# Computing the last 64 tokens of four sequences from two matmuls on a block-diagonal layout of their weights

## The chip, the cores and the metric

The kernel runs on one core of a Trainium2 chip. Time is the device time of one execution in microseconds (us); times given for a kernel are the median of several executions. A profile shows one execution; its span is the time from the first to the last recorded instruction. Engines are called as in the profile: PE (TensorE matmuls; PEld are its weight loads), DVE (VectorE), ACT (ScalarE), POOL (GpSimd) and SP (SyncE, which here issues DMAs).

## The reference, cut to what matters

A gated recurrence over four sequences of 5056 tokens with 256 channels is followed by a soft mixture of experts over all 20224 tokens, with 8 experts of 4 slots each (32 slots).

```python
sig = 1.0 / (1.0 + np.exp(-f_logit))
f = lower_bound + (1.0 - lower_bound) * sig
for t in range(S):
    h = f[:, t] * h + (1.0 - f[:, t]) * x[:, t]
    y[:, t] = h
...
logits = x @ phi                            # x is y as (20224, 256); 32 slots
d = softmax of logits over the tokens       # slot inputs: d.T @ x
slot_out[e] = np.maximum(slot_input[e] @ w1[e], 0.0) @ w2[e]
c = softmax of logits over the 32 slots
return c @ slot_out                         # (20224, 256), float32
```

What the change touches is the last line, for the last 64 tokens of each sequence.

## The kernel before

Everything is laid out by hand; each engine executes its instructions in the order in which the source issues them.

**Stage 1 (to about 120 us)** streams `x` and `f_logit` in units of one sequence by 512 tokens (`load`, L210), computes gates on ACT, their products with x on POOL, transposes on PE, and the recurrence as scans on DVE (L319). Logits come out of PE with the slots on the partitions: partition `32 b + s` holds slot s of sequence b. Their exponentials lie in `etall`, 128 partitions by 5056 tokens, in bf16 (L120). PE also adds up the slot inputs (`slot_ps`).

**Stage 2 (to about 144 us)** runs the experts while the last weights arrive through POOL's DMA queue (`load_w`, L135). Among this, `row_sums` (L394) adds the 32 exponentials of each token with matmuls against `ones`, whose first four columns hold ones on the 32 partitions of one sequence each and whose other columns are all ones. The sums go into PSUM and their reciprocals into `rrow`. Matmuls that only keep PE busy (`spin`, `narrow`, L150 to L159) stand at several places. The last operations of the stage form `slot_out` (L750), the expert outputs with slots on partitions, repeated for the four sequences; `slot_bd` (L759), made of it on POOL, has two column halves of 256, in which every other sequence's rows are zero.

**Stage 3 (from 143.5 us)** multiplies the exponentials by the expert outputs, scales each row by its reciprocal sum, and stores. The tokens of a sequence are cut into `blocks`: two of 2048 tokens (16 a partition) and one of 896 (7 a partition); 64 tokens are left over (`L`). Three early rows are stored first (`total` and `early`, L753 to L757). Then follow `pieces` for the first block of the last sequence, `whole` and `couple` for the last block, `rest` for the left-over tokens, and `whole` and `couple` for the other blocks (L853 to L863). `couple` handles two sequences in one matmul of 512 columns; DVE and ACT take turns in scaling (`by_vector`, `by_scalar`). All stores are issued by SP in this order. Tiles `ob` and `oc` have three buffers each; a fourth use waits for the store of the first.

The left-over tokens before: `left_over` (L406) copies each sequence's last 64 columns of `etall` into `left`, 64 tokens by 2, where the second index is the sequence's parity and the other half stays zero. `rest` (L836) does two matmuls, one for each pair of sequences, over 64 partitions and 512 columns. Each leaves two halves, which ACT copies and DVE adds, so that partition `2 t + u` holds token t of one of the two sequences. One DVE instruction then scales both, and SP issues two stores with one row of 256 values (1 KB) a partition. Their row sums are one matmul against `pair_ones` (L402).

Of the kernel before, what the change touches and what calls it, by code (L numbers as in the profile page):

```python
# [9 lines left out]
F32 = mybir.dt.float32  # L10
BF16 = mybir.dt.bfloat16
AX = mybir.AxisListType
ALU = mybir.AluOpType
# [5 lines left out]
def kernel(  # L19
# [10 lines left out]
    nc = tc.nc  # L30
    B, S, D = x.shape
    E = moe_w1.shape[0]
    F = moe_w1.shape[2]
    NS = moe_phi.shape[1]
    SPE = NS // E
    P = 128
    DC = D // P
    FC = F // P
    R = 4
    G = P * R  # L40
    n_grp = (S + G - 1) // G
# [15 lines left out]
    L = used(odd) - P * R3  # L57
# [9 lines left out]
    consts = ctx.enter_context(tc.tile_pool(name="consts", bufs=1))  # L67
# [20 lines left out]
    ones = consts.tile([P, P], BF16, name="ones")  # L88
# [2 lines left out]
    for b in range(B):  # L91
        nc.vector.memset(ones[ds(b * NS, NS), ds(b, 1)], 1.0)

    pair_ones = consts.tile([P, B // 2], BF16, name="pair_ones")
    nc.vector.memset(pair_ones, 0.0)
    for j in range(B // 2):
        nc.vector.memset(pair_ones[ds(j * 2 * NS, 2 * NS), ds(j, 1)], 1.0)

    parity = consts.tile([P, 2], F32, name="parity")
    nc.vector.memset(parity, 0.0)  # L100
    for b in range(B):
# [16 lines left out]
    store = ctx.enter_context(tc.tile_pool(name="store", bufs=1))  # L118
    PAD = 48
    etall = store.tile([P, S + PAD], BF16, name="etall")[:, :S]  # L120
    rrow = store.tile([P, n_grp * R, B], F32, name="rrow")
    left = store.tile([P, L, 2], BF16, name="left")
    nc.vector.memset(left, 0.0)
    csum = store.tile([P, n_grp], F32, name="csum")
    nc.vector.memset(csum, 0.0)
# [2 lines left out]
    slot_bd = store.tile([P, 2, D], BF16, name="slot_bd")  # L128
    slot_out = store.tile([P, D], BF16, name="slot_out")
# [25 lines left out]
    def narrow(dst, k):  # L155
        for i in range(k):
            nc.tensor.matmul(dst[ds(i % B * NS, NS), ds(0, D)], w1_sb[0][:, 0, ds(0, NS)],
                             w1_sb[0][:, 0, ds(0, D)], start=True, stop=True,
                             skip_group_check=True)  # L159
# [8 lines left out]
    with tc.tile_pool(name="sp2", bufs=3) as sp2, \  # L168
# [225 lines left out]
        def row_sums(i):  # L394

            t0, n_r = blocks[i]
            ew = etall[:, ds(t0, P * n_r)].rearrange("s (p r) -> s p r", r=n_r)
            for r in range(n_r):
                nc.tensor.matmul(sums[:, ds((t0 // P + r) * B, P)], ew[:, :, r], ones,
                                 start=True, stop=True, skip_group_check=True)  # L400
            if i == len(blocks) - 1:
                nc.tensor.matmul(rs_ps[:, n_grp * R - 1, ds(0, B // 2)],  # L402
                                 left.rearrange("s t u -> s (t u)"), pair_ones,
                                 start=True, stop=True, skip_group_check=True)

        def left_over():  # L406
            for b in range(B):
                k = ds(b * NS, NS)
                nc.gpsimd.tensor_copy(left[k, :, b % 2], etall[k, ds(S - L, L)])

        def slots(g):
            n_p = rows(g)
# [72 lines left out]
        for n in range(n_unit):  # L485
# [14 lines left out]
            else:  # L500
# [40 lines left out]
                if n == n_unit - 2:  # L541
                    tail = psp.tile([P, 2, G], F32, name="tail", tag="sp")
                    sums = tail[:, 0]
                    rs_ps = sums[:, ds(0, n_grp * R * B)].rearrange(
                        "p (q b) -> p q b", b=B)
# [44 lines left out]
        slots(odd)  # L590
        late_slots()
        spin(tail[:, 1], 2, D)
        narrow(tail[:, 1], 8)
        slot_sb = hpool.tile([P, G, DC], BF16, name="slot_sb", tag="h")
        slot_sb = slot_sb.rearrange("p t o -> p (t o)").bitcast(F32)[:, ds(0, D)]
        nc.vector.tensor_copy(slot_sb, slot_ps)
# [2 lines left out]
        for o in range(DC):  # L599
            nc.tensor.matmul(sin_ps[:, o], slot_v[:, o], rep[:, 0],  # L600
                             start=True, stop=True, skip_group_check=True)
# [3 lines left out]
    with tc.tile_pool(name="ew", bufs=1) as ew, \  # L605
# [116 lines left out]
        nc.vector.tensor_copy(total, sum_ps)  # L722
        k = len(blocks) - 1
        nc.vector.reciprocal(rrow[:, k * wide_r:q], rs_ps[:, k * wide_r:q])
        nc.vector.reciprocal(rrow[:, q, ds(0, B // 2)], rs_ps[:, q, ds(0, B // 2)])
        nc.tensor.matmul(so_ps, rep2, total, start=True, stop=False, skip_group_check=True)

        def last_chunk(fc):
# [34 lines left out]
    with tc.tile_pool(name="osb", bufs=3, reuse_waits="tile") as osb:  # L763

        def by_vector(ob, op, scale):
            nc.vector.tensor_tensor(ob, op, scale.broadcast_to(list(ob.shape)), ALU.mult)  # L766

        def by_scalar(ob, op, scale):
            for i in range(ob.shape[1]):
                nc.scalar.activation(ob[:, i], op[:, i], ACT.Copy, scale=scale[:, i])  # L770

        def share(op, i, b, r, k):
            t0, n_r = blocks[i]
            ew = etall[ds(b * NS, NS), ds(t0, P * n_r)].rearrange("s (p r) -> s p r", r=n_r)
            for j in range(k):
                nc.tensor.matmul(op[:, j], ew[:, :, r + j], slot_out[ds(b * NS, NS)],  # L776
                                 start=True, stop=True, skip_group_check=True)

        def scale_of(i, b, r, k):
            return rrow[:, ds(blocks[i][0] // P + r, k), ds(b, 1)]  # L780

        def rows_of(i, b):
            t0, n_r = blocks[i]
            return out[ds(b * S + t0, P * n_r)].rearrange("(p r) d -> p r d", r=n_r)

        pout = ctx.enter_context(
            tc.tile_pool(name="pout", bufs=8, space=PSUM, reuse_waits="tile"))

        def bank():
            return pout.tile([P, 2, D], F32, name="op", tag="op")  # L790

        def pieces(i, b):
            dst = rows_of(i, b)
            ob = osb.tile([P, blocks[i][1], D], F32, name="ob", tag="ob")
            for r, ks in ((3, (1, 1)), (5, (1, 1)), (7, (1, 1)), (9, (2, 2)), (13, (2, 1))):
                q = r
                for k, by in zip(ks, (by_vector, by_scalar)):
                    op = bank()
                    share(op, i, b, q, k)
                    by(ob[:, ds(q, k)], op[:, ds(0, k)], scale_of(i, b, q, k))  # L800
                    q += k
                nc.sync.dma_start(out=dst[:, ds(r, q - r)], in_=ob[:, ds(r, q - r)])

        turn = [0]

        def next_engine():
            turn[0] += 1
            return turn[0] % 2

        def whole(i, b):  # L810
            n_r = blocks[i][1]
            ob = osb.tile([P, n_r, D], F32, name="ob", tag="ob")
            for r in range(0, n_r, 2):
                k = min(2, n_r - r)
                op = bank()
                share(op, i, b, r, k)
                (by_scalar, by_vector)[next_engine()](
                    ob[:, ds(r, k)], op[:, ds(0, k)], scale_of(i, b, r, k))
            nc.sync.dma_start(out=rows_of(i, b), in_=ob)

        def couple(i, j):
            t0, n_r = blocks[i]
            ew = etall[ds(j * 2 * NS, 2 * NS), ds(t0, P * n_r)].rearrange(
                "s (p r) -> s p r", r=n_r)
            ob = osb.tile([P, 2, n_r, D], F32, name="oc", tag="oc")
            for r in range(n_r):
                op = bank()
                nc.tensor.matmul(op.rearrange("p u d -> p (u d)"), ew[:, :, r],  # L828
                                 slot_bd[ds(j * 2 * NS, 2 * NS)].rearrange("s u d -> s (u d)"),
                                 start=True, stop=True, skip_group_check=True)  # L830
                (by_scalar, by_vector)[next_engine()](
                    ob[:, :, r], op, rrow[:, t0 // P + r, ds(2 * j, 2)].unsqueeze(2))
            for u in range(2):
                nc.sync.dma_start(out=rows_of(i, 2 * j + u), in_=ob[:, u])

        def rest():  # L836
            n_p = B // 2
            ob = osb.tile([P, n_p, D], F32, name="ob", tag="ob")
            dst = out.rearrange("(b t) d -> t b d", b=B)
            for j in range(n_p):  # L840
                k = ds(j * 2 * NS, 2 * NS)
                op = bank()
                nc.tensor.matmul(op.rearrange("p u d -> p (u d)"),
                                 left[k].rearrange("s t u -> s (t u)"),
                                 slot_bd[k].rearrange("s u d -> s (u d)"),
                                 start=True, stop=True, skip_group_check=True)
                nc.scalar.copy(ob[:, j], op[:, 0])
                nc.vector.tensor_tensor(ob[:, j], ob[:, j], op[:, 1], ALU.add)
            by_vector(ob, ob, rrow[:, n_grp * R - 1, ds(0, n_p)].unsqueeze(2))
            for j in range(n_p):  # L850
                nc.sync.dma_start(out=dst[ds(S - L, L), ds(2 * j, 2)], in_=ob[:, j])

        pieces(0, B - 1)  # L853
        end = len(blocks) - 1
        whole(end, 0)
        whole(end, 1)
        couple(end, 1)
        rest()
        whole(0, B - 2)
        for i in range(end):  # L860
            for j in range(B // 2):
                if i or j < B // 2 - 1:
                    couple(i, j)  # L863
# [30 lines left out]
```

## Time and profile before

| | |
|---|---|
| median of 3 runs | 197.58 us (197.51 to 197.93) |
| the profiled execution | 197.61 us, span 195.8 us |
| busy share of the span | PE 77%, DVE 75%, ACT 72%, POOL 52% |
| mean granted PE clock | 0.857 of full |
| read from and written to HBM | 58.23 MB and 20.71 MB |
| first store issued / last store packet starts | 143.50 us / about 193.4 us |

The page gives each engine's busy time, the span in 40 slices of 4.9 us, the chain of work that ended last, groups of instructions by source line and operand, and the DMA issues with size and the time until they had landed. A group reads: line, engine, operation, output and inputs, partitions by elements, count, busy time, mean. The trace behind the page also answers for stretches of time (busy time of each engine, clock, DMA share and GB/s), as a timeline, and by tile. A DMA store or load is split into packets of one contiguous run each, spread over 16 DMA engines.

Where tiles lie in a partition is fixed when the program is built; tiles are rounded up to 32 bytes. The tiles that matter, in bytes from the partition's start:

| tile | before | after |
|---|---|---|
| `pair_ones` (4 bytes used) | 19488 | none |
| `etall` | 19552 | 19520 |
| `left` | 30400, 256 bytes | 30368, 512 bytes |
| `slot_out` | 31744 | 31968 |
| `w1_sb0` | 32256 | 32480 |
| `f_t`, first buffer | 89600 | 89824 |
| `x_t`, first buffer | 114176 | 114400 |
| `ob` of `pieces` | 65024 | 65248 |
| `oc`, first buffer | 81408 | 81632 |
| `total` | 147680 | 147904 |
| `early` | 148704 | 148928 |

All buffers of `f_t`, `x_t`, `w1_sb`, `w2_sb`, `ob` and `oc` start on multiples of 512 before, and 224 bytes past one after. 48 unused columns of bf16 (`PAD`, L119) stand behind `etall` in both.

### The profile page before, as it was taken

The page shows a single profiled execution, that of the slowest core. Times are in us where ns is not written, and L with a number is a line of the kernel's source. Part 1 is how long each engine was busy: PE and PEld are TensorE (multiplying, and loading weights), DVE is VectorE, ACT ScalarE, POOL GpSimd, SP SyncE. Part 2 cuts the span into 40 slices and gives each one's busy share as a digit, 9 for nine tenths or more (in the row PEclk, how much of TensorE's full clock was granted, in tenths as well). Part 3 has the DMA queues.
Part 4 walks back from the last instruction along what each step waited for, and adds up shares of the span by engine and source line. Part 5 has one row for each costly group of instructions (what it writes and reads, how often), then busy time and mean ns, then how long its engine had stood idle before and what let it go on. Part 6 is the DMA issues. An engine that isn't in the chain of part 4 may idle for free.

```text
span 195.8 us, 3290 instructions
## 1 busy us (share of the span) xinstructions
PE 151.2 (77%) x1209; PEld 105.9 (54%) x1209; DVE 145.9 (75%) x188; ACT 141.6 (72%) x198; POOL 101.5 (52%) x79
## 2 busy tenths in 40 slices
PE   0589498987998979899797987998889999950000
PEld 0367377775785757667585766556573533410000
DVE  2669869989699999999999999544289888950000
ACT  3698687799889998999987799434089799960000
POOL 2489578874997789874969979253030000000000
PEclk9999979998799999999999999999995555555555
DMA  5999999999999999999999999999949999999994
GB/s 203 395 419 421 428 428 423 425 428 365 372 428 427 408 327 427 420 421 340 369 420 421 260 215 213 214 213 214 172 180 417 425 430 428 425 432 442 435 442 181
DMA packets 14305, 70.75 MB, mean 361 GB/s; under 512 B 1601, under 2 KB 2882, under 8 KB 10322
## 3 DMA queue, kind: packets, MB, share of 16 engines
q1 hardware_dynamic: 11520, 62.13, 76.5%
q0 software_dynamic: 2768, 8.42, 21.7%
q8 instruction: 9, 0.15, 0.3%
q14 instruction: 6, 0.05, 0.1%
q10 hardware_dynamic: 2, 0.00, 0.0%
HBM read 58.23 MB, written 20.71 MB: 403 GB/s over the span
## 4 chain that ended last, share of the span: by engine, by line
PE 33%; DMA 23%; DVE 18%; POOL 7%; issue 5%; ACT 2%; SPq 0%; POOLq 0%; ACTq 0%; DVEq 0%
DMA x_t<-in_x_dram 15%; DVE h L319 13%; PE op L828 11%; DMA w_sb<-in_moe_w_dram 9%; POOL u_t L252 6%; PE hp L332 4%; PE up L273 3%; DVE ht L351 3%; PE sp L267 3%; PE op L776 3%; PE lg L365 2%; PE slot_ps L189 2%; POOL w_sb L147 1%; DVE et L389 1%; ACT ob L770 1%
## 5 line engine op out<-in xcount | busy, mean ns | idle before, releaser
L252 POOL TENSOR_TENSOR u_t<-s_t,x_t 128x1024 bf16<-128x1024 bf16 (+1 forms) x39 | 82.5, 2131 | 22.8 <-ACT s_t L241 13.5
L319 DVE TENSOR_TENSOR_SCAN h<-a,h,up 128x512 bf16<-128x512 f32 (+1 forms) x72 | 86.8, 1252 | 5.1 <-PE up L273 2.9
L241 ACT ACTIVATE s_t<-f_t 128x2048 bf16<-128x2048 f32 (+2 forms) x23 | 38.3, 1668 | 4.8 <-DMA f_t<-in_f_logit_dram 4.8
L332 PE MATMUL hp<-ident_f,h 128*128 128x128 f32 (+1 forms) x160 | 29.7, 311 | 8.2 <-DVE ht L351 6.8
L332 PEld LDWEIGHTS hp<-ident_f,h 128*128 128x128 f32 (+1 forms) x160 | 23.5, 207 | 18.8 <-DVE ht L351 13.2
L267 PE MATMUL sp<-ident_f,s_t 128*128 128x128 f32 x144 | 23.0, 307 | 6.5 <-ACT s_t L241 4.6
L301 ACT ACTIVATE a<-sp,lbs 128x1024 f32<-128x1024 bf16 x24 | 25.4, 1115 | 1.1 <-PE sp L267 1.0
L267 PEld LDWEIGHTS sp<-ident_f,s_t 128*128 128x128 f32 x144 | 18.6, 158 | 8.4 <-ACT s_t L241 5.2
L828 PE MATMUL op<-slot_bd,etall 64*128 64x512 bf16 x55 | 22.7, 626 | 0.0
L770 ACT ACTIVATE oc<-op,rrow 128x256 f32<-128x256 f32 x54 | 21.4, 505 | 0.2
L766 DVE TENSOR_TENSOR oc<-op,rrow 128x512 f32<-128x512 f32 x28 | 18.8, 688 | 3.3 <-PE op L828 3.2
L308 ACT ACTIVATE a<-sp,lbs 128x512 f32<-128x512 bf16 (+2 forms) x22 | 17.8, 858 | 4.6 <-PE sp L267 4.2
L273 PE MATMUL up<-ident_f,u_t 64*128 64x64 f32 x192 | 17.9, 232 | 2.1 <-POOL u_t L252 2.1
L273 PEld LDWEIGHTS up<-ident_f,u_t 64*128 64x128 f32 x192 | 14.2, 141 | 6.1 <-POOL u_t L252 2.5
L189 PE MATMUL slot_ps<-rep,ident_f 128*128 128x256 f32 x52 | 16.9, 419 | 0.0
L351 ACT COPY ht<-hp 128x512 f32<-128x512 f32 (+1 forms) x20 | 11.7, 583 | 5.6 <-PE hp L332 5.5
L828 PEld LDWEIGHTS <-etall 64*128 64x128 bf16 x55 | 8.3, 158 | 13.4 <-issue 12.9
L351 DVE COPY ht<-hp 128x512 f32<-128x512 f32 (+1 forms) x20 | 13.3, 667 | 0.8 <-PE hp L332 0.8
L319 DVE TENSOR_TENSOR_SCAN h<-a,up 128x512 bf16<-128x512 f32 x8 | 9.4, 1211 | 2.8 <-ACT a L308 1.9
L267 PE MATMUL up<-ident_f,u_t 128*128 128x128 f32 x48 | 9.5, 331 | 0.8 <-POOL u_t L252 0.8
L365 PE MATMUL lg<-h,phi 128*32 128x512 bf16 (+1 forms) x80 | 9.4, 389 | 0.3 <-ACT et L389 0.2
L189 PEld LDWEIGHTS slot_ps<-rep,ident_f 128*128 128x128 f32 x52 | 8.3, 194 | 1.6 <-issue 0.6
(132 smaller groups left out, 154.1 us busy)
## 6 DMA issues: line engine op xcount, KB each, us to landing
f_t<-in_f_logit_dram SPq DMA_DIRECT2D x12, 1024.0 KB, 12.1
x_t<-in_x_dram SPq DMA_DIRECT2D x12, 1024.0 KB, 11.5
out_dram<-oc SPq DMA_DIRECT2D x6, 2048.0 KB, 12.3
w_sb<-in_moe_w_dram POOLq DMA_DIRECT2D x14, 512.0 KB, 10.2
f_t<-in_f_logit_dram SPq DMA_DIRECT2D x12, 512.0 KB, 8.5
x_t<-in_x_dram SPq DMA_DIRECT2D x12, 512.0 KB, 9.7
out_dram<-ob SPq DMA_DIRECT2D x1, 2048.0 KB, 9.2
out_dram<-ob SPq DMA_DIRECT2D x2, 896.0 KB, 5.6
```

The costliest lines, as they stand in the source:

```text
L189: nc.tensor.matmul(slot_bank[:, 1], ident_f, wide_rep, start=False, stop=False, skip_group_check=True)
L241: nc.scalar.activation(s_t, f_t, ACT.Sigmoid, scale=-1.0)
L252: nc.gpsimd.tensor_tensor(uts[n][:, :r], s_t[:, :r], x_t[:, :r], ALU.mult)
L267: nc.tensor.transpose(ps[:, :, r], t[:, r], ident_f)
L273: nc.tensor.transpose(v[:, :, r], t(r)[k].bitcast(F32), ident_f[k, k])
L301: nc.scalar.activation(a, sp[:, :, :, :, o], ACT.Identity, scale=nomlb[:, ds(o, 1)], bias=1.0)
L319: nc.vector.tensor_tensor_scan(h[:, :T, o], decays[n // 2, o][:, n % 2, :T], up[:, :T, o], hs[number(g - 1, b)][:, ds(used(g - 1) - 1, 1), ...
L332: nc.tensor.transpose(hp[:n_p, r], hw[:, :n_p, r], ident_f)
L351: copy(hts[g][:n_p, b].rearrange("p r d -> p (r d)").bitcast(F32), hps.pop(n)[:n_p].rearrange("p r c -> p (r c)"))
L766: nc.vector.tensor_tensor(ob, op, scale.broadcast_to(list(ob.shape)), ALU.mult)
L770: nc.scalar.activation(ob[:, i], op[:, i], ACT.Copy, scale=scale[:, i])
L828: nc.tensor.matmul(op.rearrange("p u d -> p (u d)"), ew[:, :, r], slot_bd[ds(j * 2 * NS, 2 * NS)].rearrange("s u d -> s (u d)"), start=Tru ...
```

## The change

`left` becomes 128 partitions by 2 by 32 by 4: for each parity r of the token, 32 tokens by 4 sequences, where partition `32 b + s` is filled only at index b. So one matmul over all 128 partitions against `slot_out` gives, for token parity r, the outputs of 32 tokens of all four sequences, with token and sequence on the partitions: partition `4 t + b`. Two matmuls of 256 columns (r = 0 and 1) fill both halves of one PSUM bank, one DVE instruction scales them, and one store writes 2 KB, two neighbouring tokens, from each partition. Nothing is left to be added, so ACT's copies and DVE's additions go, and `rest` no longer reads `slot_bd`. The row sums are two matmuls against column B of `ones` (a column of all ones) in place of one against `pair_ones`, which goes with its memsets. POOL's copies in `left_over` read every other token. One of eight `narrow` matmuls behind the slot inputs goes.

```diff
-    pair_ones = consts.tile([P, B // 2], BF16, name="pair_ones")
-    nc.vector.memset(pair_ones, 0.0)
-    for j in range(B // 2):
-        nc.vector.memset(pair_ones[ds(j * 2 * NS, 2 * NS), ds(j, 1)], 1.0)
...
-    left = store.tile([P, L, 2], BF16, name="left")
+    left = store.tile([P, 2, L // 2, B], BF16, name="left")
     nc.vector.memset(left, 0.0)
...
             if i == len(blocks) - 1:
-                nc.tensor.matmul(rs_ps[:, n_grp * R - 1, ds(0, B // 2)],
-                                 left.rearrange("s t u -> s (t u)"), pair_ones,
-                                 start=True, stop=True, skip_group_check=True)
+                for r in range(2):
+                    nc.tensor.matmul(rs_ps[:, n_grp * R - 1, ds(r, 1)],
+                                     left[:, r].rearrange("s t b -> s (t b)"),
+                                     ones[:, ds(B, 1)],
+                                     start=True, stop=True, skip_group_check=True)
...
-                nc.gpsimd.tensor_copy(left[k, :, b % 2], etall[k, ds(S - L, L)])
+                nc.gpsimd.tensor_copy(left[k, :, :, b], etall[k, ds(S - L, L)].rearrange(
+                    "s (t r) -> s r t", r=2))
...
-        narrow(tail[:, 1], 8)
+        narrow(tail[:, 1], 7)
...
-        nc.vector.reciprocal(rrow[:, q, ds(0, B // 2)], rs_ps[:, q, ds(0, B // 2)])
+        nc.vector.reciprocal(rrow[:, q, ds(0, 2)], rs_ps[:, q, ds(0, 2)])
...
         def rest():
-            n_p = B // 2
-            ob = osb.tile([P, n_p, D], F32, name="ob", tag="ob")
-            dst = out.rearrange("(b t) d -> t b d", b=B)
-            for j in range(n_p):
-                k = ds(j * 2 * NS, 2 * NS)
-                op = bank()
-                nc.tensor.matmul(op.rearrange("p u d -> p (u d)"),
-                                 left[k].rearrange("s t u -> s (t u)"),
-                                 slot_bd[k].rearrange("s u d -> s (u d)"),
+            ob = osb.tile([P, 2, D], F32, name="ob", tag="ob")
+            op = bank()
+            for r in range(2):
+                nc.tensor.matmul(op[:, r], left[:, r].rearrange("s t b -> s (t b)"), slot_out,
                                  start=True, stop=True, skip_group_check=True)
-                nc.scalar.copy(ob[:, j], op[:, 0])
-                nc.vector.tensor_tensor(ob[:, j], ob[:, j], op[:, 1], ALU.add)
-            by_vector(ob, ob, rrow[:, n_grp * R - 1, ds(0, n_p)].unsqueeze(2))
-            for j in range(n_p):
-                nc.sync.dma_start(out=dst[ds(S - L, L), ds(2 * j, 2)], in_=ob[:, j])
+            by_vector(ob, op, rrow[:, n_grp * R - 1, ds(0, 2)].unsqueeze(2))
+            dst = out.rearrange("(b t) d -> b t d", b=B)[:, ds(S - L, L)]
+            nc.sync.dma_start(out=dst.rearrange("b (t r) d -> t b (r d)", r=2),
+                              in_=ob.rearrange("p r d -> p (r d)"))
```

## The prediction, made before the changed kernel had run

> **What bounds the kernel now.** I read the windows by stage first, because a share over the whole span mixes stages. The columns after the engines are granted clock, busy share of the 16 DMA engines and GB/s moved.
>
> ```profile
> 0.70:34.60 33.90, 23.67 (x130) 18.81 (x131) 25.00 (x44) 24.60 (x27) 22.80 (x18) 0.95 0.97 396
> 34.60:110.00 75.40, 67.92 (x618) 52.38 (x618) 71.61 (x69) 68.85 (x66) 60.08 (x34) 0.98 1.02 396
> 119.50:142.00 22.50, 20.09 (x296) 13.19 (x294) 11.41 (x22) 8.83 (x18) 8.30 (x16) 1.00 1.04 204
> 145.00:193.40 48.40, 28.83 (x91) 12.41 (x87) 26.36 (x42) 28.27 (x75) 0.73 (x1) 0.52 1.01 425
> ```
>
> The DMA engines are full in the loads (to 110 us), in the weights (119 to 142) and in the stores (145 to 193.4). In the store stage no compute engine is busy for more than 0.60 of the time (PE, 28.83 of 48.40). So whatever the changed `rest` saves in compute there is worth nothing unless it changes what the DMA engines do. Next the timeline of the edited place:
>
> ```profile
> 150.39 0.63 PE L843 MATMUL op<-slot_bd,left 64*128 64x512 bf16 x1
> 150.93 0.65 ACT L847 COPY ob<-op 128x256 f32<-128x256 f32 x2
> ...
> 152.12 0.69 DVE L766 TENSOR_TENSOR ob<-ob,rrow 128x512 f32<-128x512 f32 x1
> 152.76 3.03 ACT L770 ACTIVATE ob<-op,rrow 128x256 f32<-128x256 f32 x8 [1.18 <-DMA out_dram<-ob]
> 153.08 2.56 SPq L851 DMA_DIRECT2D out_dram<-ob  x2
> ```
>
> After `rest`, ACT waits 1.18 us for an earlier `ob` store to land: the next rows are held by the stores, not by `rest`. Its own 1 KB packets move only at 158.5 to 159.5, 5.7 us after issue, behind queued stores.
>
> Last, the rates of single stores:
>
> ```profile
> 144.50:144.70 0.20, 0.20 (x4) 0.20 (x3) 0.20 (x1) 0.20 (x2) 0.20 (x1) 1.00 1.00 333
> 145.15:145.65 0.50, 0.50 (x8) 0.50 (x7) 0.50 (x2) 0.50 (x3) 0.50 (x1) 1.00 1.02 385
> 146.00:146.50 0.50, 0.34 (x4) 0.34 (x4) 0.50 (x2) 0.50 (x3) 0.00 (x0) 1.00 1.06 406
> 146.50:147.00 0.50, 0.50 (x5) 0.42 (x4) 0.50 (x2) 0.50 (x2) 0.00 (x0) 0.56 1.10 426
> 147.00:147.50 0.50, 0.50 (x4) 0.11 (x2) 0.50 (x2) 0.50 (x3) 0.00 (x0) 0.50 1.03 397
> 158.60:159.10 0.50, 0.50 (x2) 0.16 (x1) 0.34 (x2) 0.50 (x3) 0.00 (x0) 0.50 1.05 367
> ```
>
> These are, in order, `total` (1 KB packets), `early` (2 KB), three windows of `pieces` (2 KB) and `rest` (1 KB). `total` and `early` start 224 bytes past a multiple of 512 in their partition (147680 and 148704); all `ob` tiles start on a multiple of 512. Time per packet on one engine is 16 x bytes / rate. For 2 KB it is 85.1 ns in `early` against 79.9 ns in `pieces` (mean 410 GB/s); for 1 KB it is 49.2 ns in `total` against 44.6 ns in `rest`. Both pairs differ by about 5 ns, on the same side.
>
> **The change part by part.** The profiled execution took 197.61 us (span 195.8, so 1.8 around it); the median is 197.58. I add to 197.6.
>
> *Row sums (L402).* One more 128x128 weight load and matmul stand between the row sums and the chain `so_ps`, `slot_out`, first store. The load takes 0.10 us (140.41 to 140.51), and PE takes up L726 at 140.62, when `total` is just there (DVE L722 ends at 140.56). The second load fits that gap; its matmul may push L726. Between 0 and 0.17 us (L402's own matmul); I take 0.05, by the row sums of L399 at 1.22 us for 16.
>
> *One narrow matmul fewer (L157).* 0.05 us of PE at 128 us (8 in 0.40). PE then waits 1.18 us for weights at 137.87, which hides it; without that cover, -0.05. The clock is granted at 1.00 from 126.08 to 146.56 in every stretch, even with PE busy 2.23 of 3.41 us, so I price a clock loss at nothing.
>
> *Constants and POOL.* `pair_ones` loses three DVE memsets (0.06 + 0.17 us) and the memset of `left` doubles from 0.11 us, all before 2.5 us; DVE then waits 2.71 us for x_t. The four POOL copies (258 ns each, from 133.0) now read with a step of 2. At 258 to twice that they end by 135.1, and the first reader is at 140.41. All nothing.
>
> *`rest` itself.* PE goes from 2 x 0.43 us to 2 x 0.23 (16 rows of L776 in 3.63); ACT loses 0.65, DVE 0.75, SP one issue of 1.28. The following rows still wait at 152.76 for the same store, so ACT's wait becomes 1.8 us in place of 1.18. `whole(0, 2)` is then issued at 155.8 as now, after its last ACT row. The first matmul no longer needs `slot_bd` but `slot_out`, ready since 143.7. Nothing; were the DMA backlog gone, at most the 0.75 of DVE would show.
>
> *Its store.* 16 packets of 1 KB per engine (16 x 44.6 = 0.71 us) become 8 of 2 KB: 8 x 79.9 = 0.64, or 8 x 85.1 = 0.68 off the multiple. In a full queue this counts: -0.03 to -0.07; I take -0.03.
>
> *What is not in the diff's lines: addresses.* Dropping `pair_ones` frees 32 bytes a partition and `left` grows from 256 to 512, so every tile allocated behind it moves by +224. Before, in the program's layout, f_t, x_t, w1_sb, w2_sb, `ob` and `oc` all start on multiples of 512 (f_t 89600, `ob` 65024, `oc` 81408); after, all stand 224 past one, exactly where `early` stands now. `total` and `early` go from 224 to 448 and stay off.
>
> Store packets behind `early`, per engine (a store of 128 rows gives each of the 16 engines 8): `pieces` five stores, 40; the last block four stores of 7 KB rows, 32; the other blocks seven stores of 16 KB rows, 56. Together 128, and at 5 ns 0.64 us. Bounds: 0 (the two slow stores were the first in an empty queue) and 5.2 x 128 = 0.67; no misaligned 7 or 16 KB packet is in the trace. I take 0.64, because two sizes show the same extra.
>
> Here a page bears on it. The Trainium skill, "DMA: Bandwidth & Descriptors", section "How a descriptor splits into AXI transactions", says that a transaction starts on a 256 B boundary, so an unaligned descriptor begins below its start and pays for unused 32 B beats. At 224 these are 7 beats; at 79.9 ns for the 64 beats of 2 KB that is an estimated 8.7 ns, 1.1 us over 128 packets, and 198.7 by the same sum. The trace agrees in sign, with 5 ns in place of 8.7; its 198.7 lies in the first case's own range below. Whether writes into the core pay too the section does not say.
>
> Loads write to the shifted addresses; no row shows an off-multiple load. From the issue list each engine has 192 packets of 8 KB, 192 of 4 KB, 64 of 3 KB and 32 of 1 KB, 480 in all: 0 to 480 x 5.2 = 2.5 us. A misaligned start was seen only where the core is read, so I take 0 and keep 2.5 as the bound. The weight packets (4 KB cast to bf16) take twice a plain one because twice the bytes are read; 0 too.
>
> Sum: 197.6 + 0.05 - 0.03 + 0.64 = 198.3.
>
> **The rivals.**
>
> *Loads pay as well.* For it: the load stage runs at a DMA share of 0.97 and 1.02, so nothing hides a slower packet. Against: no row, and DVE is nearly as full (71.61 of 75.40). 197.6 + 0.66 + 2.5 = 200.8 at most, half of the loads' part 199.5.
>
> *Addresses cost nothing.* The 5 ns would be the start of an empty queue, and longer packets would hide it. Then 197.6 + 0.05 - 0.07 = 197.6, no change.
>
> *Faster: the last engine catches up.* The end is set by one DMA engine that is one packet behind:
>
> ```profile
> 193.00:193.20 0.20, 0.00 (x0) 0.00 (x0) 0.00 (x0) 0.00 (x0) 0.00 (x0) 0.50 0.00 0
> 193.20:193.40 0.20, 0.00 (x0) 0.00 (x0) 0.00 (x0) 0.00 (x0) 0.00 (x0) 0.50 0.23 82
> ```
>
> 82 GB/s in 0.2 us is one packet of 16 KB that starts alone; it takes about 0.6 us (16 engines at 427 GB/s). One 8 KB instruction packet moves at 144.8, just as the stores begin, and holds one engine about 0.3 us. Four ACT, three DVE and one SP instruction fewer may move that fetch before the stores or onto another engine. If that engine is the late one and addresses cost nothing, the end comes up to 0.6 us sooner, 197.1 with jitter of the rest. It decides from the moment that the fetch leaves the stretch after 144.3. Against: most of the removed instructions stand behind it.
>
> That the change does not shorten `rest` is not at issue: the instructions are gone in the program as built.
>
> **How the numbers follow.** Stores pay: 0.40, own range 197.9 to 198.8. Loads pay too: 0.20, 199.0 to 200.8. No change: 0.22. Faster: 0.18. The measurement can tell about 0.2% (0.4 us) from no change. Slower by more is the second case and nearly all of the first, 0.58; within, 0.24; faster, 0.18. Range 197.1 to 200.0: it cuts half of the fastest case and about half of the loads' case. Predicted 198.3.
>
> **What would show it.** Right: the stage that ends with the last store moves its 20.5 MB at about 419 GB/s in place of 425 (48.4 us becomes 49.0), single 16 KB packets about 5 ns longer, and the first store at 143.5 plus 0.05; DVE's work for `rest` is one 0.69 us instruction, ACT waits 1.8 us before its next rows. The loads' rival: 396 GB/s falls to about 388 before 110 us, and everything behind comes later by the loss. No change: rates as now. Faster: no packet that starts alone at the end. I am wrong if store rates are equal and the time still moves, or if PE's clock falls before 143.

## The result, and the profile after

| | before | after |
|---|---|---|
| median of 6 runs each, in turn on one chip | 197.56 us (197.38 to 197.93) | 198.97 us (198.81 to 199.20) |
| ratio, 95% interval | | 1.0071 [1.0061, 1.0082] |
| profiled execution, span | 197.61 us, 195.8 us | 198.81 us, 197.0 us |
| first store issued | 143.50 us | 144.82 us |
| last packet of a store ends | 194.0 us | 195.8 us |
| from there to the end of the span | 1.80 us | 1.24 us |

The change costs 1.4 us. The last three rows split the 1.2 us of the two profiled executions into three parts: the stores begin 1.32 us later, take 0.48 us longer from first issue to last packet, and the end behind them is 0.56 us shorter. (That a packet of a store ends at 194.0 or 195.8 is read from the packet records of the trace.)

The windows by stage of the kernel after, with the columns of before (busy time of PE, PEld, DVE, ACT and POOL, granted clock, DMA share, GB/s); the store window is moved by the 1.32 us:

```profile
0.70:34.60 33.90, 23.62 (x132) 17.38 (x132) 24.92 (x41) 24.52 (x27) 23.13 (x18) 0.95 0.99 393
34.60:110.00 75.40, 66.94 (x601) 51.52 (x602) 69.54 (x67) 67.15 (x64) 57.77 (x32) 0.95 1.02 395
119.50:142.00 22.50, 20.54 (x302) 13.79 (x300) 13.22 (x22) 11.15 (x22) 10.88 (x17) 1.00 1.06 210
146.32:194.72 48.40, 27.66 (x91) 12.40 (x87) 25.25 (x40) 26.66 (x73) 0.72 (x1) 0.54 1.02 423
```

GB/s in the loads fall from 396 to 393 and 395. In the third window the engines did more than before (DVE 13.22 us against 11.41, POOL 10.88 against 8.30): the same work as before, come later. The stores move 423 GB/s against 425. No window shows a break; the loss is spread over the loads.

The edited place, in the timeline after (start, length, engine, line, operation, count; in brackets the wait ahead of it and what ended it):

```profile
150.76 0.59 PE L838 MATMUL op<-slot_out,left 128*128 128x256 bf16 x2
...
152.51 0.69 DVE L764 TENSOR_TENSOR ob<-op,rrow 128x512 f32<-128x512 f32 x1
...
154.23 1.20 SPq L842 DMA_DIRECT2D out_dram<-ob  x1
154.62 0.84 ACT L768 ACTIVATE ob<-op,rrow 128x256 f32<-128x256 f32 x2 [2.45 <-DMA out_dram<-ob]
```

`rest` does what the diff says: two matmuls, one DVE instruction of 0.69 us, one store, nothing on ACT. What ACT saves it spends waiting: 2.45 us for an earlier store of `ob` to land, where it was 1.18.

The row sums, just ahead of the path to the first store:

```profile
141.46 0.42 DVE L720 COPY total<-sum_ps 128x256 f32<-128x256 f32 x1 [0.39 <-PE sum_ps L668]
...
141.79 0.19 PE L398 MATMUL tail<-ones,left 128*128 128x1 bf16 x2
141.94 0.70 PE L724 MATMUL so_ps<-total,rep 128*128 128x256 f32 x2
```

`total` is ready at 141.88 and L724, which needs it, starts at 141.94, as the two row-sum matmuls end. Before, the same matmul (L726 there) started as long behind `total`, which was ready at 140.56:

```profile
140.62 0.70 PE L726 MATMUL so_ps<-total,rep 128*128 128x256 f32 x2
```

So the second row-sum matmul fits in front of it. But all of this stands 1.32 us later than before, as much as the first store: the time was lost ahead of the row sums.

The end, in windows:

```profile
194.60:194.80 0.20, 0.00 (x0) 0.00 (x0) 0.00 (x0) 0.00 (x0) 0.00 (x0) 0.50 2.89 1229
194.80:195.00 0.20, 0.00 (x0) 0.00 (x0) 0.00 (x0) 0.00 (x0) 0.00 (x0) 0.50 0.00 0
195.00:195.20 0.20, 0.00 (x0) 0.00 (x0) 0.00 (x0) 0.00 (x0) 0.00 (x0) 0.50 0.19 82
```

A packet is counted where it starts: fifteen of the last sixteen start in one window, and one alone, 82 GB/s, as before. So here too one DMA engine ends late, at 195.80 us, 0.4 us behind the others (before: 0.5 us).

### The profile page after: what moved, and what is told of

It is laid out like the page before. It is cut to its first block, busy times and chain, and to the rows that moved or that the text cites. A ratio compares the mean times of both kernels' runs of the same rounds, so it can differ in the third digit from the quotient of the medians.

```text
span 197.0 us, 3282 instructions
## 1 busy us (share of the span) xinstructions
PE 151.2 (77%) x1209; PEld 105.2 (53%) x1209; DVE 145.0 (74%) x183; ACT 139.9 (71%) x196; POOL 102.1 (52%) x79
## 4 chain that ended last, share of the span: by engine, by line
DMA 33%; PE 26%; DVE 14%; POOL 8%; issue 5%; ACT 2%; SPq 0%; POOLq 0%; ACTq 0%; DVEq 0%
DMA x_t<-in_x_dram 15%; DVE h L314 10%; PE op L826 10%; DMA w_t<-in_moe_w_dram 9%; DMA f_t<-in_f_logit_dram 7%; POOL u_t L247 6%; PE hp L327 4%; PE up L268 3%; DMA out_dram<-ob 3%; PE sp L262 3%; DVE ht L346 2%; PE slot_ps L184 2%; POOL w_sb L142 2%; ACT ob L768 1%; PE lg L360 1%
## 5 line engine op out<-in xcount | busy, mean ns | idle before, releaser
L262 PE MATMUL sp<-ident_f,s_t 128*128 128x128 f32 x144 | 22.2, 299 | 7.4 <-ACT s_t L236 4.7
L262 PEld LDWEIGHTS sp<-ident_f,s_t 128*128 128x128 f32 x144 | 17.9, 154 | 9.6 <-ACT s_t L236 5.6
L826 PE MATMUL op<-slot_bd,etall 64*128 64x512 bf16 x55 | 21.6, 598 | 0.7 <-DVE ob L764 0.5
L768 ACT ACTIVATE oc<-op,rrow 128x256 f32<-128x256 f32 x54 | 20.3, 566 | 0.0
L268 PE MATMUL up<-ident_f,u_t 64*128 64x64 f32 x192 | 18.7, 237 | 2.1 <-POOL u_t L247 1.9
L268 PEld LDWEIGHTS up<-ident_f,u_t 64*128 64x128 f32 x192 | 14.7, 145 | 6.4 <-POOL u_t L247 2.5
L184 PE MATMUL slot_ps<-rep,ident_f 128*128 128x256 f32 x52 | 17.5, 433 | 0.2 <-POOL rep L86 0.2
```

Of the source, the lines that this page charges most:

```text
L184: nc.tensor.matmul(slot_bank[:, 1], ident_f, wide_rep, start=False, stop=False, skip_group_check=True)
L262: nc.tensor.transpose(ps[:, :, r], t[:, r], ident_f)
L268: nc.tensor.transpose(v[:, :, r], t(r)[k].bitcast(F32), ident_f[k, k])
```

## The experiments

All were run beside the kernel before, whose medians on the four chips used were 197.51, 197.55, 197.57 and 197.60 us. Ratios are to those, with 95% intervals. The theory was that the +224 bytes cost and the new work doesn't; the rivals were that only the stores pay, that only the loads pay, or that the new code costs.

### Take the shift away from the change, and give it to the kernel before

After, with `left` and the rest as changed, and 32 more unused bytes behind `etall`, so that all large tiles stand at 256 past a multiple of 512:

```diff
-    PAD = 48
+    PAD = 64
```

> The changed kernel with 16 more unused columns behind etall (PAD 64 for 48): 32 bytes, so that f_t, x_t, w1_sb, w2_sb, ob and oc start 256 past a multiple of 512, that is on a multiple of 256, instead of 224 past it. If the shifted addresses make the 1.4 us: 197.4 to 197.8, as the kernel before. If the work of the change (row sums, one narrow matmul fewer, the new rest) makes it: 198.9 to 199.1, as the changed kernel. If only a multiple of 512 will do: 199 as well, and then b1 is still slow.

Measured 197.02 us, 0.9974 [0.9963, 0.9984]. The change with other addresses is faster than before. Against the change as it stands (1.0071) that is 1.9 us for 32 unused bytes.

Before, with all that lies behind `etall` moved by +224, and by +64:

```diff
-    PAD = 48
+    PAD = 160
```

```diff
-    PAD = 48
+    PAD = 80
```

> The kernel before with PAD 160 for 48: every tile behind etall lies 224 bytes higher, where the changed kernel has them; nothing else differs. Addresses: 198.8 to 199.2 (plus 1.4). Work of the change: 197.4 to 197.7, no change.

> The kernel before with everything behind etall 64 bytes higher (PAD 80). If a packet pays whenever it starts off a multiple of 256: plus 1.2 to 1.8, 198.7 to 199.3, with 8 KB load packets at 312 ns or more for 309. If only an odd multiple of 32 pays (224 is one): 197.4 to 197.7.

Measured 199.22 us, 1.0082 [1.0069, 1.0095], and 199.05 us, 1.0080 [1.0067, 1.0092]. So addresses alone, with no line of computation touched, cost 1.5 to 1.7 us; +64 costs what +224 does, while a1's multiple of 256 costs nothing. An offset of 128 was not tried. The Trainium skill, "DMA: Bandwidth & Descriptors", section "How a descriptor splits into AXI transactions", puts the line at 256 B too, and there the runs agree. The section speaks of reads; the loads here write into the core, and the stores read it. By an estimate from its count of unused beats, 7 at +224 and 2 at +64, the second should cost under a third of the first; the runs show no such difference, in the time or in the stores alone (a 16 KB store packet takes 611.5 ns before, 617.3 in b1 and 617.0 in b5).

### Loads, stores or compute

Before, with an unused tile ahead of one pool, so that only some tiles move. Ahead of the load buffers (b2: `f_t`, `x_t` and the compute tiles are moved; weights, `ob` and `oc` are not), behind them (b4: compute tiles alone, by the first two lines below put one line further down), ahead of the store buffers (b3: `ob` and `oc` alone):

```diff
+    gap0 = held.enter_context(tc.tile_pool(name="gap0", bufs=1))
+    gap0.tile([P, 56], F32, name="gap0")
```

```diff
+    gap2 = ctx.enter_context(tc.tile_pool(name="gap2", bufs=1))
+    gap2.tile([P, 56], F32, name="gap2")
```

> The kernel before with a gap of 224 bytes ahead of the load buffers: f_t, x_t and the compute tiles behind them are shifted, weights and the store tiles ob and oc are not. If both loads and stores pay: plus 0.6 to 1.0, 198.2 to 198.6. If only reads from the core pay (the prediction's first case): 197.5 to 197.7. If loads alone make all: 198.9.

> The kernel before with a gap of 224 bytes ahead of ob and oc alone: only the stores of the last stage read off a multiple of 256. The prediction's first case: 128 packets an engine times 5 ns, plus 0.64: 198.1 to 198.3. If longer packets hide it: 197.5 to 197.7.

> The kernel before with a gap of 224 bytes behind the load buffers: f_t, x_t, weights, ob and oc stay on multiples of 512, only the compute tiles (s_t, u_t, a, h, ht, et and the later ones) are shifted. If the load packets that write off a multiple make the 1.7 us of the two shifted kernels: 197.4 to 197.7, no change. If the engines' accesses to shifted tiles make it: 198.9 to 199.3.

| moved by +224 | median | ratio |
|---|---|---|
| everything (b1) | 199.22 us | 1.0082 [1.0069, 1.0095] |
| load buffers and compute (b2) | 199.25 us | 1.0083 [1.0070, 1.0096] |
| compute alone (b4) | 197.58 us | 1.0002 [0.9993, 1.0011] |
| store buffers alone (b3) | 197.59 us | 1.0004 [0.9995, 1.0013] |

The loads are the whole of it, as far as the intervals (0.26 us) can tell: b1, which moves weights and stores as well, is no longer than b2. The stretch from 7 to 20 us, where the loads have 4 KB packets and the queue is full, shows it in one number, the last of each line (GB/s). Before, after, a1, b2 and b3, in this order:

```profile
7.00:20.00 13.00, 10.26 (x51) 8.15 (x50) 10.25 (x11) 10.97 (x15) 10.87 (x9) 1.00 1.02 419
```

```profile
7.00:20.00 13.00, 9.62 (x51) 7.09 (x50) 10.47 (x11) 10.62 (x15) 10.82 (x9) 1.00 1.03 410
```

```profile
7.00:20.00 13.00, 9.86 (x51) 7.44 (x50) 10.65 (x11) 10.72 (x16) 11.12 (x9) 1.00 1.02 419
```

```profile
7.00:20.00 13.00, 10.42 (x50) 8.20 (x49) 10.46 (x11) 10.84 (x15) 10.89 (x9) 1.00 1.03 412
```

```profile
7.00:20.00 13.00, 10.00 (x52) 7.66 (x50) 10.52 (x12) 10.88 (x15) 11.08 (x9) 1.00 1.03 420
```

At the same DMA share, 410 and 412 where both load buffers are off a multiple of 256, 419 and 420 where they aren't. So it is in all fourteen kernels profiled: 408 to 412 in the four with both off (after, b1, b2, b5), 419 to 422 in the other ten. The packet records of the trace say the same. The median load packet of 4 KB takes 159 ns and that of 8 KB 309 ns in each of the ten; 162 and 313 in after, b1 and b2; 161 and 312 in b5. (The means are less clear, since a few packets take several times as long.) All loads together hold each DMA engine for 99.9 us before, 101.9 after, 101.5 in b1, 101.4 in b2, 101.0 in b5, 100.0 in b3, 99.7 in b4 and 100.1 in a1. Since the queue is full, the weights behind the loads come later, and the first store with them. The timeline of SP, first store, in before, after, b2, b3 and a1:

```profile
143.50 0.35 SPq L754 DMA_DIRECT2D out_dram<-total  x1
```

```profile
144.82 0.35 SPq L752 DMA_DIRECT2D out_dram<-total  x1
```

```profile
145.22 0.35 SPq L756 DMA_DIRECT2D out_dram<-total  x1
```

```profile
143.53 0.35 SPq L754 DMA_DIRECT2D out_dram<-total  x1
```

```profile
143.28 0.35 SPq L752 DMA_DIRECT2D out_dram<-total  x1
```

The store packets do get longer in b3, 611.5 to 617.3 ns for 16 KB, 272.6 to 278.5 for 7 KB and 85.0 to 87.8 for 2 KB: 0.7 us more for each engine (49.06 to 49.78). The windows of b3 show the store stage and its last round:

```profile
145.00:193.40 48.40, 27.88 (x91) 12.32 (x88) 26.05 (x42) 27.39 (x75) 0.77 (x1) 0.53 1.01 420
193.20:193.40 0.20, 0.00 (x0) 0.00 (x0) 0.00 (x0) 0.00 (x0) 0.00 (x0) 0.50 0.00 0
193.40:193.60 0.20, 0.00 (x0) 0.00 (x0) 0.00 (x0) 0.00 (x0) 0.00 (x0) 0.50 2.50 1065
```

420 GB/s against 425, as predicted for stores that pay. But no packet starts alone at the end any more. Before, fifteen engines were done at 193.24 to 193.50 us and one at 194.00; in b3 all sixteen end at 194.06 to 194.25. The fifteen use up the time in which they used to wait for the sixteenth, and the last packet ends 0.25 us later. The sixteenth does not end 0.7 us later, as its own longer packets would make it: in b3 it is no longer late, and why is open. By the median the kernel is 0.08 us longer (interval: -0.1 to +0.26).

In the kernel after, one engine stays late, and the stores take 0.48 us longer from first issue to last packet (b1 0.38, b5 0.49, b3 0.22; but a1 0.26 and d1 0.35 with stores on the boundary). In the four kernels with shifted stores the time from the last packet to the end is in turn about 0.14 us shorter than in the others with as many DMAs. What is left for the stores lies within the intervals.

### Only one of the two load streams

Before, with `x_t` alone moved (to 480 past a multiple of 512), and with `f_t` alone at 64 (`x_t` at 256): gaps of 40 and 16 columns between the two buffers, and for the second an unused tile of 16 columns ahead of the pool.

```diff
+                    if n == 0 and tag == "x_t":
+                        ld.tile([P, 40], F32, name="gap3", tag="gap3")
```

> The kernel before with a gap of 480 bytes between the buffers of f_t and those of x_t: half of the load packets, those of x, write 224 past a multiple of 256, those of f_logit do not; weights, ob and oc do not either. If each shifted load packet pays on its own: half of the 1.7 us, 198.2 to 198.6. If a stretch of the schedule tips over as a whole: 197.5 or 199.2.

> The kernel before with the buffers of f_t 64 past a multiple of 256 and those of x_t, weights, ob and oc on one (the later compute tiles on one too). All at 64 cost 1.5 us. If each off-multiple load packet pays alike, and x at 480 (32 below a multiple of 512) was nearly free for its own offset: half, 198.2 to 198.5. If the loads of f_logit alone set the pace and those of x are free wherever they lie: 198.8 to 199.2. If both must be off for a cost: 197.5 to 197.8.

Measured 197.75 us, 1.0022 [1.0009, 1.0036], and 197.76 us, 1.0007 [0.9994, 1.0020]. Half of the cost, the first case of both, did not come: by the ratios, one stream off the boundary costs 0.4 or 0.1 us, not half of 1.7. For `f_t` it is the third case, that both must be off. Two of the twelve executions with `x_t` moved took 198.7 and 199.1 us, near the time of the full shift, and the other ten 197.65 to 197.83; why is open (a single one of 198.7 or 198.8 us stands among those of b7 and of the kernel before, too). The stretch from 7 to 20 us moves what it moves before, in b6 and b7:

```profile
7.00:20.00 13.00, 10.58 (x52) 8.26 (x50) 10.54 (x12) 10.87 (x15) 11.12 (x9) 1.00 1.03 421
```

```profile
7.00:20.00 13.00, 10.49 (x51) 8.46 (x50) 10.43 (x12) 10.78 (x15) 10.98 (x9) 1.00 1.02 419
```

84% and 90% of the 8 KB packets take 309 ns in them, against 92% before and 33% in b2. So most packets of the moved stream keep their length, too.

### The change without its shift: where does a1's gain come from?

a1 is 0.5 us faster than before. It has one DMA fewer on the hardware queues: 80 in place of 81. In the program as built these take eight completion semaphores in turn, and SP's last waits go through the eight in a fixed order. With 81, the last store falls on the first of them, and seven waits still follow when it lands; with 80 it falls on the last. To tell this from the smaller store and the shorter `rest`: a1 with its store in two halves (81 again), and before with one small load, `lb_row`, issued by POOL (80).

```diff
-            nc.sync.dma_start(out=dst.rearrange("b (t r) d -> t b (r d)", r=2),
-                              in_=ob.rearrange("p r d -> p (r d)"))
+            for r in range(2):
+                nc.sync.dma_start(out=dst.rearrange("b (t r) d -> r t b d", r=2)[r],
+                                  in_=ob[:, r])
```

```diff
-    nc.scalar.dma_start(out=lb_row, in_=lower_bound.unsqueeze(0))
...
+    nc.gpsimd.dma_start(out=lb_row, in_=lower_bound.unsqueeze(0))
```

> The changed kernel realigned (PAD 64), with the store of rest split in two stores of 1 KB rows, so that the kernel has as many SP DMAs as before. The DMA semaphores are used in turn, eight of them, and SP's last waits go through them in order: with 81 DMAs the last store is on the first and seven waits follow it, with 80 it is on the eighth and none follows. If the realigned kernel is 0.5 us faster than the one before by these waits: 197.4 to 197.6. If by the work that rest saves: 197.0 to 197.1.

> The kernel before with the 1 KB load of lower_bound issued by POOL instead of ACT, so that the DMAs counted on the eight semaphores are 80 as in the changed kernel and the last store is on the eighth. Waits at the end: 197.0 to 197.2. If the changed rest or row sums make the difference: 197.4 to 197.7.

Measured 197.57 us, 1.0003 [0.9994, 1.0012], and 197.14 us, 0.9978 [0.9967, 0.9989]. With 81 DMAs the realigned change is the kernel before, to 0.1%; with 80, the kernel before gains 0.4 us. SP's waits (waited for, us in total, times, longest) show the order at work, in before, c1, after and c2:

```profile
SPq L889 <- DMA out_dram<-oc: 18.0, 1, 18.0
```

```profile
SPq L882 <- DMA out_dram<-oc: 18.3, 1, 18.3
```

```profile
SPq L881 <- DMA out_dram<-oc: 18.4, 4, 4.9
```

```profile
SPq L889 <- DMA out_dram<-oc: 17.7, 4, 4.8
```

With 81 the wait on the last store, ahead of the seven others, lasts until it has landed (once, 18.0 us); the seven find their stores long done but are still gone through afterwards. In the trace's records of SP before, the wait for the last store is passed at 194.49 us and the last of the seven at 194.92, 0.43 us later; in c2 none stands behind it. With 80 the waits follow the stores as they land, four waits of up to 4.9 us, and the last to land is the last waited for. From the last packet to the end of the span the nine profiled kernels with 81 took 1.66 to 1.82 us (mean 1.77), the five with 80 took 1.24 to 1.40 (mean 1.36). The 0.56 us that the kernel after gains here are these 0.43 and the 0.14 or so that go with its shifted stores.

### Two more parts of the change

a1 with the `narrow` matmul put back, and a1 with `total` and `early`, which are off the boundary in a1, brought to a multiple of 512 by an unused tile ahead of them:

```diff
-        narrow(tail[:, 1], 7)
+        narrow(tail[:, 1], 8)
```

```diff
+        ew.tile([P, 8], F32, name="gap4")
```

> The changed kernel realigned (PAD 64), with eight narrow matmuls again for seven. As the prediction has it, the one matmul is hidden behind the wait for weights: 196.9 to 197.2, as the realigned kernel. If it was on the path: 0.05 more; if the granted clock hung on it: 0.5 or more either way.

> The changed kernel realigned (PAD 64), and total and early moved to a multiple of 256 as well, so that every large transfer starts on one. The two early stores have 16 packets an engine at about 5 ns: at most 0.08 us less than the realigned kernel, 196.9 to 197.1; if they do not set the pace of the last stage: 197.0.

Measured 196.96 us, 0.9974 [0.9964, 0.9984], and 197.20 us, 0.9981 [0.9972, 0.9989]. Neither differs from a1's 0.9974 by more than the intervals: the removed matmul was hidden, and two store sources off the boundary cost nothing that shows (of 0.08 us at most, which is less than the intervals can tell).

## Why the prediction was right, and where it was wrong

The time moved the way that was forecast, 1.4 us slower against 0.7, and the cause was the forecast one: not the lines of the diff, but the +224 bytes that they give to every tile behind `left`. The side was wrong: the cost was put on the stores and is on the loads. With the loads at nothing and a store term that is not paid, the sum comes to no change. That the forecast was near is so in part luck: 0.64 that was not paid stood in for 1.6 of the loads less 0.4 that nobody had foreseen.

- *The step that failed* is "A misaligned start was seen only where the core is read, so I take 0" for the loads. The likeliest case put the loss on the stores and nothing on the loads; the runs put 1.5 to 1.7 us on the loads (b2, b1, b5) and 0.08 us on the stores (b3, interval -0.1 to +0.26). The bound that was kept, 480 packets by 5.2 ns, 2.5 us, held: the engines' load time grew by 1.1 us (b5) to 2.0 us (after), 2 to 4 ns a packet. That no row showed a misaligned load was a gap in the trace, and a gap is no zero. The rival "loads pay as well" had the mechanism, and its 199.5 was half a microsecond from the result, but it carried the stores' 0.64 us, which is not paid.
- *Stores, 0.64 us.* The price came out and its effect didn't: in b3 each engine's stores take 0.7 us longer, 5.8 ns on a 16 KB packet. The price was read at 1 and 2 KB from rates, partly on a queue just filling; the packet records show 2.8 ns at 2 KB (85.0 to 87.8), so that 5 ns held for 7 and 16 KB was not in the rows it was read from. What covers it is in part what the prediction showed in its rival "the last engine catches up": the end is set by one late engine, and the other fifteen had about 0.5 to 0.75 us to spare. The late engine and the longer packets stood in the same text but not in one sum. That the late engine is on time in b3 is not explained.
- *A term that was missing:* one DMA fewer shortens the wait chain behind the last store by 0.4 us (c1, c2). It is all of the merged store's gain that shows; the 0.03 us by packet length can't be seen (c1 stands at 1.0003 with two stores).
- *Confirmed at nothing:* the row sums fit ahead of L724 (0 for 0.05); one `narrow` fewer (c3); `rest`'s compute, whose gain became ACT's wait for the store (2.45 us where 1.8 was foreseen, and 2.03 to 2.46 us in c1, a1 and d1, so it is not the shifted addresses that make it longer); the weights (b1 is no longer than b2); the constants, as c1 equals before with all of this in it.
- *What was to show it:* the store rate of 419 GB/s came out as 423, near the 425 of before, and the first store came 1.32 us later, not 0.05. That is close to the prediction's own sign of being wrong, equal store rates and a time that still moves. The loads' sign, 388 GB/s before 110 us, did not come: 393 and 395. That sign was badly chosen: in the second of these stretches a1 and b4, which lose nothing, have 394, and b5, which loses 1.5 us, has 396. The rate in a stretch with a full queue and one size of packet (419 to 410) is the sign that holds.

The sum by the runs: 1.6 us for the addresses (b1, 0.82%) less 0.4 for the end waits (c2, 0.22%) makes 1.2; measured 1.4 [1.2, 1.6]. From after against a1 the addresses come to 1.9 us. Both gaps, 0.2 and 0.3 us, lie within the intervals.

The version that beats both is a1, the change with 32 bytes more of padding: 197.02 us, 0.9974 [0.9963, 0.9984]. Most of its gain can be had in the kernel before without the change (c2, 0.9978); the difference lies within the intervals.

## What to carry to other kernels

When a change adds, drops or resizes a small tile, compare the start addresses of all large DMA buffers before and after, loads first: here a multiple of 256 bytes was worth 0.8% of the kernel, and a few bytes of padding restore it. Price a longer packet at the engine that ends last, not at the mean engine: here 0.7 us more on every engine moved the last packet by 0.25. Where several DMAs are to be awaited at the end, let the last to land be the last in the order of the waits; here that was worth 0.4 us.

## What the runs showed of the hardware that was not expected

- Load packets, which write into the core's memory, take 2 to 4 ns more when both load buffers start 64 or 224 bytes past a multiple of 256. The median of 4 KB goes from 159 to 161 (+64) and 162 ns (+224), that of 8 KB from 309 to 312 and 313 ns, and the whole kernel loses nearly the same at both offsets (1.0080 and 1.0082).
- The cost isn't additive: by the ratios, `x_t` alone off the boundary costs 0.4 us and `f_t` alone 0.1, both together 1.6. The 480 of `x_t` in b6 lies only 32 bytes short of a multiple of 512, and whether that matters was not tried; `f_t`'s 64 in b7 is an offset that costs fully in b5, where `x_t` has it too. Why both must be off was not found out.
- The seven waits on completion semaphores that stand behind that for the last store cost about 0.4 us (0.43 in the trace of before), by their order alone: in c2 they are over before it lands.
- One DMA engine runs late in the stores of the kernel before: its 16 KB packets take 614 to 653 ns until about 176 us, shortly after the computation ends, then as long as the others' 611. In b3 no engine stands out: long packets are spread over all sixteen. The prediction's guess, an instruction fetch of 8 KB on that engine, was not tried; the cause is open.
- The time does not go with the granted clock here: executions of the kernel before at a mean of 0.849 and of 0.878 took 197.48 and 197.51 us.
